# Two more ways to ScalarE and new weights for a planned instruction order (attention, FFN and gated FFN on one core)

## The chip, the cores and the metric

The kernel runs on one core of a Trainium2 chip. The metric is the device time of one execution in microseconds (us). The core has a matrix engine (TensorE: PE for its matmuls, PEld for its weight loads), and three engines for elementwise work: VectorE (DVE), ScalarE (ACT) and GpSimd (POOL). All transfers are issued from SyncE's queue (SP).

## The reference

Three layers follow each other, in double or single precision as the inputs come:

```python
# attention: q, k, v are (2, 8, 768, 64), proj is (64, 6)
mask   = bucket(q @ proj > 0) == bucket(k @ proj > 0)      # 6 sign bits make a bucket
scores = where(mask, q @ k.T / 8, -1e9)
attn   = exp(scores - max);  attn /= attn.sum(-1) + 1e-9
x      = attn @ v                                          # then (1536 tokens, 512)
# FFN 1: w_in (512, 2048), w_out (2048, 512)
h = x @ w_in;  g = max(h, 0) + log1p(exp(-abs(h)));  y = g @ w_out
# FFN 2: w_gate, w_val (512, 1536), w_out (1536, 512)
g = y @ w_gate;  out = (g * sigmoid(g) * (y @ w_val)) @ w_out
```

## The kernel before

**Chunks.** The 1536 tokens are cut into four chunks of 384 tokens: batch 0 gives chunks 0 and 1, batch 1 gives chunks 2 and 3. Attention goes head by head; a visit of a head and a chunk is three tiles of 128 queries by 768 keys. When a chunk's eight heads are done its x is split, turned by transfers and given to FFN 1 (`ffn1`, 16 blocks of 128 columns of w_in, then four blocks of y). FFN 2 (`ffn2`) comes last, for all chunks. Products are taken as three f16 matmuls of high and low parts, so nearly every tensor is split into `hi` and `lo` on the elementwise engines. The weights come as 64-bit numbers and are converted in pieces: three integer passes on DVE (lines 394, 399, 405), a square for the scale (432), high part (438 or 444) and low part (448). There are 8 pieces of w_in, 8 of w_out, 12 of w_gate and w_val, 6 of the last w_out.

**A tile of attention** (`units_of`). PE makes the scores and the mask in one product (776). `mx` on DVE copies them to SBUF and takes their maximum (787), and then works out the offset of the exponent in one element a row, `st[1] = st[0] * inv + 2` (792). `ex` on ACT takes the exponential with this offset (797). In chunk 0 (kind F, 24 tiles) the result is turned on PE (831), copied by ACT or DVE (862) and multiplied in f32 (870). In the other chunks (kind D, 72 tiles) it is split into `hi` (ACT 804, POOL 812 or DVE) and `lo` (817, POOL or DVE), turned by a transfer (PT<-P), and multiplied (854).

**Before a head's tiles** come three squares of k, q and v for their scales (`scales`: on ACT line 644, on DVE line 647), the split, the transfer that turns k and q, a copy of 64 rows (`cp`), and the hash bits (`planes`): a small product (574) whose signs become plus or minus the mask's constant, either in one DVE instruction (585), or with a Sign on ACT (594) and then an offset on POOL (599).

**FFN 1's block**: 12 matmuls into a bank of PSUM `f` (two of them in turn for batch 0); ACT takes the magnitude (`mag`, 1044), DVE the positive part (`relu`, 1049), ACT an exponential and a logarithm (1055, 1058), DVE adds (1061), then comes the split of g (ACT 1066 or POOL 1072; 1075). The bank is free when `mag` and `relu` have read it.

**The order is planned.** The program does not write its instructions in a fixed order. Each operation is a `Step` with an urgency (smaller is sooner) and one or several `ways`; a way is an engine, a length and sometimes a weight. `Order.run` plays the steps out with those lengths and emits them as it goes, and each engine then executes its own instructions in the order in which they were emitted. Three rules of it matter here:

```python
way = min(s.ways, key=lambda w: at(w) + (w[1] if w[0] != "D" else sum(w[1]) + 2.2) + (w[3] if len(w) > 3 else 0.0))
...
if w[0] in "WG":
    f += self.PORT * max(0.0, free.get("port", 0.0) - f)
...
(f for f in found if unit(f[2][0]) == unit(best[2][0]) and f[0] <= best[0] + self.SLACK),
key=lambda f: (f[1], f[0]),
```

A step takes the way with the smallest sum of start, length and weight. "V" and "W" are both DVE; a "W" or "G" (POOL) way is also pushed back by 0.75 of the time for which the plan holds the memory port of DVE and POOL taken (`PORT`). Among steps that could start on an engine within 0.1077 us of the earliest (`SLACK`), the most urgent goes first. The lengths are short formulas: with n elements a row, `dve(n)` = 0.08 + n/960, `stt(n)` = 0.13 + n/960, `act(n)` = 0.28 + n/1400, `gts(n)` = 0.05 + n/1050, `gps(n)` = 0.1 + n/510 us. `BV` holds the weights, `U` shifts of urgency, `GAP` the planned distance of tiles, `LEAD` how far ahead of its first tile a head's preparation is due, `W1_GAP` and `W2_GAP` the distance of the pieces of w_in and w_out.

Of the kernel before, what the change touches and what calls it, by code (L numbers as in the profile page):

```python
# [183 lines left out]
def tile_hash_attention__softplus_ffn__silu_glu(  # L184
# [51 lines left out]
    def pe(cols):  # L236
        return 0.04 + cols / 2400.0

    BV = dict(tf=1.0, th=1.091, hi=2.161, lo=0.772, slo=0.117, wlo=-0.43, bits=0.477, meas=0.564, cv=-0.593, ca=0.872)
    U = dict(vl=0, tp=-2.89, th=-2, tl=-2, w2=53.21, qp=-7.63, kp=-4.93, kv=3.56, f1=0, y=40, ev=-9.89, ex=3.56, hi=-7.89, lo=2.67, gw=423.98, x=2.84)  # L240

    const = ctx.enter_context(tc.tile_pool(name="const", bufs=1))
    xyp = ctx.enter_context(tc.tile_pool(name="xyp", bufs=1))
# [33 lines left out]
    def ways(urgency, opts, after=(), takes=(), uses=(), line=None):  # L277
        return order.step(urgency, opts, after, takes, uses, line)
# [357 lines left out]
    def scales(b, h, u, kv, ld_kv, qr, ld_q):  # L636

        n = NT * D
        m, x, inv = small(3), small(3), small(2)
        e = e_hd[b][:, 3 * h:3 * h + 3]  # L640
        src = (lambda: kv[0].t, lambda: qr.t, lambda: kv[1].t)

        def measure_a(i):
            return lambda: nc.scalar.activation(junk, src[i](), AF.Square, accum_out=m[:, i:i + 1])

        def measure_v(i):
            return lambda: nc.vector.scalar_tensor_tensor(
                out=junk2, in0=src[i](), scalar=1.0, in1=src[i](), op0=ALU.mult, op1=ALU.mult,
                accum_out=m[:, i:i + 1],
            )  # L650

        def least():
            nc.vector.scalar_tensor_tensor(
                out=e, in0=bank_.t[:, 8:11], scalar=2.0 ** 51, in1=floors, op0=ALU.mult, op1=ALU.max
            )

        def inverse():
            for i, c in enumerate((QK_SC, -QK_SC)):
                nc.vector.tensor_scalar(
                    inv[:, i:i + 1], e[:, 0:1], e[:, 1:2], c, op0=ALU.mult, op1=ALU.mult  # L660
                )
        ms = [
            ways(u, [("A", act(n) + 0.15, measure_a(i)), ("V", stt(n) - 0.07, measure_v(i), BV["meas"])],
                 [ld], uses=[o])
            for i, (ld, o) in enumerate(((ld_kv[0], kv[0]), (ld_q, qr), (ld_kv[1], kv[1])))
        ]
        s, bank_ = total(u, m, 3, ms)
        s = es = step(u, "W", 0.55, both(
            lambda: half_bits(bank_.t[:, 8:11], bank_.t[:, 0:3]), least, lambda: two_over(x, e)
        ), [s], uses=[bank_])  # L670
        iv = step(u + 5, "V", 0.4, inverse, [s])
        return dict(x=x, es=es, inv=inv, iv=iv, ready=s)

    def key_side(b, h, u, hs, raw, ld, proj_ready):

        nat, kk = Slot("natk"), Slot("k")
        n = NT * D

        def parts():
            if nat.t is None:  # L680
                new(att, [128, NT, 128], F16, nat)
            return (raw[0].t.rearrange("p (t d) -> p t d", d=D), nat.t[:, :, 0:64], nat.t[:, :, 64:128],
                    hs["x"][:, 0:1])

        def trans():
            a = new(att, [128, 2, NT * 128], F16, kk)
            nc.sync.dma_start_transpose(
                out=a[:, 0].rearrange("p (t c) -> p t c", c=128), in_=nat.t.rearrange("p t c -> p (t c)")
            )

        def copy_d():
            nc.sync.dma_start(out=kk.t[64:128, 1], in_=kk.t[0:64, 0])

        def copy_v():
            nc.vector.tensor_copy(kk.t[64:128, 1], kk.t[0:64, 0])

        def copy_a():
            nc.scalar.copy(kk.t[64:128, 1], kk.t[0:64, 0])

        g = step(u, "-", 0.0, lambda: None, [hs["ready"], ld[0]], takes=[nat], line="natk")  # L700
        lk = split(u, n, parts, [g], [raw[0], nat])
        tr = step(u, "D", (1.2, 0.95), trans, [lk], takes=[kk], uses=[nat], line="tk")
        cp = ways(u, [("W", dve(NT * 128, 4), copy_v, BV["cv"]), ("A", act(NT * 128), copy_a, BV["ca"]),
                      ("D", (0.68, 0.28), copy_d)], [tr], uses=[kk])
        pl = planes(u + U["kp"], 0, 2, lambda: kk.t[:, 0], lambda: kk.t[:, 1], [tr, proj_ready], [], [kk])
        return dict(k=kk, raw_v=raw[1], ready=[tr, cp] + pl, f_ready=ld[1])
# [13 lines left out]
    def query_side(b, h, half, u, hs, raw, ld, proj_ready):  # L720
# [22 lines left out]
        def copy_a():  # L743
# [2 lines left out]
        g = step(u, "-", 0.0, lambda: None, [hs["ready"], ld], takes=[nat], line="natq")  # L746
        lo = split(u, n, parts, [g], [raw, nat])
        tr = step(u, "D", (1.2, 0.48), trans, [lo], takes=[qq], uses=[nat], line="tq")
        cp = ways(u, [("W", dve(CN, 4), copy_v, BV["cv"]), ("A", act(CN), copy_a, BV["ca"]),
                      ("D", (0.68, 0.14), copy_d)], [tr], uses=[qq])  # L750
        pl = planes(u + U["qp"], 1, 1, lambda: qq.t[:, 0], lambda: qq.t[:, 1], [tr, proj_ready], [], [qq])
        return dict(q=qq, ready=[tr, cp] + pl)
# [6 lines left out]
    def units_of(b, h, half, due, hs, kd, qd):  # L759
# [7 lines left out]
        for t in range(HT):  # L767
# [13 lines left out]
            def mx(t=t, z=z, st=st, E=E):  # L781


                if t == 0:
                    new(att, [128, 2, HT], F32, sums)
                a = new(att, [128, 4], F32, st)
                nc.vector.tensor_scalar(  # L787
                    new(att, [128, 2, HS], F32, E), z.t[:, :, 0:HS], MASK_FLOOR, None,
                    op0=ALU.max, op1=ALU.max, accum_out=a[:, 0:1],
                )  # L790

                nc.vector.tensor_scalar(  # L792
                    a[:, 1:2], a[:, 0:1], hs["inv"][:, 1:2], E_SHIFT, op0=ALU.mult, op1=ALU.add
                )

            def ex(t=t, st=st, E=E):
# [68 lines left out]
            def apply_f(t=t, PT=PT):  # L865
# [3 lines left out]
                for kk in range(NT):  # L869
# [4 lines left out]

            s = step(u, "E", pe(4 * HS), qk, kd["ready"] + qd["ready"], takes=[z], uses=[kd["k"], qd["q"]],
                     line="qk", behind=turned[-2:-1])
            s = step(u, "V", dve(S) + 0.36, mx, [s, first, hs["iv"]],
                     takes=[st, E] + ([sums] if t == 0 else []), uses=[z] + ([sums] if t else []), line="mx")
            first = first or s
            s = x = step(u + U["ex"], "A", act(S) + 0.39, ex, [s], uses=[E, st, sums], line="ex")  # L880
            if kinds[t] == "D":
                s = ways(u + U["hi"], [("A", act(S), hi_a), ("G", gts(S) + 0.08, hi_g), ("W", dve(S, 2), hi_v, BV["hi"])], [s],
                         takes=[P], uses=[E], line="hi")
                s = ways(u + U["lo"], [("G", gps(S) + 0.05, lo(nc.gpsimd)), ("W", dve(S), lo(nc.vector), BV["lo"])], [s], uses=[E, P])
                s = step(u, "D", (1.72, 1.9), tr, [s], takes=[PT], uses=[P], line="tr")
            else:
                s = step(u + U["tp"], "E", 6 * 0.14, turn, [s], takes=[T], uses=[E], line="tp")
# [34 lines left out]
            )  # L922

        u += U["ev"]
        a = step(u, "G", 0.15, ev2a, [x], uses=[sums])
        a = step(u, "V", 0.17, ev2b, [a], uses=[sums])
        f = xn_open.get(c)
        s = step(u, "V", dve(HT * 64) + 0.07, ev3, [s, a, f], takes=[] if f else [xn[c]],
# [95 lines left out]
    def ffn1(c, due, x_ready, w1_ready, g_ready, w2_ready, y_ready):  # L1024
# [3 lines left out]
        for m in range(K1):  # L1028
# [19 lines left out]
            def relu(gi=gi, f=f, fr=fr):  # L1048
# [2 lines left out]
                    op0=ALU.mult, op1=ALU.max,  # L1051
                )

            def ex(fa=fa):
                nc.scalar.activation(fa.t, fa.t, AF.Exp, scale=-1.0)

# [23 lines left out]
                         x_ready + [w1_ready[gi], s], takes=[] if p else [f, g], uses=[f, g] if p else [], line="f1")  # L1080
            hs.append(s)
            a = step(U["f1"], "A", act(CN), mag, [s, g_ready], takes=[fa], uses=[f])
            r = step(U["f1"], "V", stt(CN) + 0.07, relu, [a, g_ready], takes=[fr], uses=[f])
            a = step(U["f1"], "A", act(CN) - 0.04, ex, [a], uses=[fa])
            a = step(U["f1"], "A", act(CN) + 0.04, ln, [a], uses=[fa])
            a = step(U["f1"], "W", stt(CN) + 0.07, add, [a, r], uses=[fa, fr])
# [116 lines left out]
    s, pm_bank = total(0, pm, 1, [s])  # L1203
    pjr = step(0, "V", 1.8, prep_proj, [s], uses=[pm_bank])

    T0, GAP, LEAD, W1_GAP, W2_GAP = 12, 2.611, 14.38, 5.974, 6.601


    visits = [(0, h, (0,), False) for h in range(H)]
# [135 lines left out]
```

## Time and profile before

| | |
|---|---|
| median of 3 runs | 885.31 us (883.08 to 885.72) |
| the profiled execution, its own time | 884.34 us |
| its span, first to last instruction | 882.5 us |
| busy of the span: PE, DVE, ACT, POOL | 779.3, 584.9, 460.3, 407.7 us |
| mean granted clock of TensorE | 0.957 of full speed |

Busy time is the time in which an engine executes an instruction, counted once where two overlap. Since the layers follow each other, a share of the whole span is a mean over stages with different limits. The time around the span (884.34 less 882.5, or 1.84 us) belongs to the execution and not to the program's instructions.

### The profile page before, as it was taken

Reading aid. Unit: us, or ns where it says so; the run is one execution under the profiler, and the core shown is the slowest. Engines: PE = TensorE matmul, PEld = TensorE weight load, DVE = VectorE, ACT = ScalarE, POOL = GpSimd, SP = SyncE. Lnnn points to the kernel's source line nnn. Section 1 sums busy time; section 2 is a strip of 40 time slices with the busy share of each in tenths; the row PEclk is TensorE's granted clock in tenths of the full one; section 3 lists DMA queues with packets and bytes.
Section 4 is the critical chain, followed back from the end, with each engine's and each line's share of the span. In section 5 each row is a group of like instructions: output and inputs, shape, how many; then the busy total and the mean of one; then the engine's idle time right before and its main releaser. Section 6 shows DMA issues by size and latency. Waiting matters only on the chain.

```text
span 882.5 us, 14634 instructions
## 1 busy us (share of the span) xinstructions
PE 779.3 (88%) x5462; PEld 505.3 (57%) x5462; DVE 584.9 (66%) x1157; ACT 460.3 (52%) x847; POOL 407.7 (46%) x430
## 2 busy tenths in 40 slices
PE   3787776877889886779999999899999999999998
PEld 1565654444445553445566666555576676677666
DVE  4798888789989899999667799968911311220320
ACT  4666667668567688767568548624411211211220
POOL 2345346877578788877348418512311210210220
PEclk9988998889879998899999999999999999999999
DMA  6445457946668787857793541342200000000000
GB/s 186 124 146 167 112 131 172 189 100 149 117 135 162 159 139 146 151 98 135 120 157 70 185 161 40 127 160 96 96 12 25 1 9 28 1 1 36 1 1 36
DMA packets 195048, 90.05 MB, mean 102 GB/s; under 512 B 156640, under 2 KB 181664, under 8 KB 194976
## 3 DMA queue, kind: packets, MB, share of 16 engines
q1 hardware_dynamic: 194976, 89.11, 43.0%
q8 instruction: 43, 0.70, 0.3%
q14 instruction: 29, 0.24, 0.1%
HBM read 47.35 MB, written 3.15 MB: 57 GB/s over the span
## 4 chain that ended last, share of the span: by engine, by line
PE 49%; DVE 22%; DMA 10%; POOL 7%; issue 6%; ACT 3%; SPq 1%; DVEq 0%; POOLq 0%; ACTq 0%
PE z L1020 8%; PE z L1022 8%; PE z L1021 8%; DMA PT<-P 4%; PE f L1183 4%; PE f L1181 4%; PE f L1182 4%; DVE E L787 3%; DVE fr L1061 2%; DMA q<-natq 2%; POOL P L817 2%; DVE fr L1049 2%; PE z L776 2%; DVE w32b L399 1%; PE y L1020 1%
## 5 line engine op out<-in xcount | busy, mean ns | idle before, releaser
L1149 DVE SCALAR_TENSOR_TENSOR sg<-z,smalls,sg 128x384 f32<-128x384 f32 x96 | 59.2, 616 | 176.9 <-ACT sg L1143 175.4
L1158 POOL TENSOR_TENSOR sT<-sg,sT 128x384 fp32r<-128x384 f32 x48 | 51.8, 1080 | 217.0 <-ACT sT L1155 211.1
L797 ACT ACTIVATE E<-E,st,smalls 128x768 f32<-128x768 f32 x96 | 98.1, 1022 | 28.0 <-DVE st L792 25.8
L776 PE MATMUL z<-k,q 128*128 128x384 f16 x384 | 87.6, 359 | 15.7 <-DVE E L787 15.4
L787 DVE TENSOR_SCALAR_CACHE_REDUCE E<-z 128x768 f32<-128x768 f32 x96 | 91.2, 950 | 9.4 <-POOL P L817 5.3
L817 POOL TENSOR_TENSOR P<-E,P 128x768 f16<-128x768 f32 x51 | 87.0, 1708 | 12.7 <-ACT P L804 9.8
L1075 POOL TENSOR_TENSOR g<-fr,g 128x384 f16<-128x384 f32 x64 | 73.6, 1154 | 16.7 <-ACT g L1066 13.1
L1020 PE MATMUL f<-xy,w1h 128*128 128x384 f16 x192 | 65.8, 343 | 10.7 <-DVE fr L1049 9.1
L854 PE MATMUL pv<-v,PT 128*128 128x64 f16 x1296 | 52.4, 197 | 19.1 <-DMA PT<-P 18.4
L854 PEld LDWEIGHTS <-PT 128*128 128x128 f16 x1296 | 47.6, 101 | 34.5 <-DMA PT<-P 27.4
L1021 PE MATMUL f<-xy,w1h 128*128 128x384 f16 x192 | 65.6, 342 | 0.0
L1022 PE MATMUL f<-xy,w1l 128*128 128x384 f16 x192 | 65.4, 341 | 0.0
L1020 PE MATMUL z<-xy,wgh 128*128 128x384 f16 x192 | 62.6, 326 | 0.7 <-DVE sg L1149 0.7
L1020 PE MATMUL z<-xy,wvh 128*128 128x384 f16 x192 | 62.6, 326 | 0.0
L1021 PE MATMUL z<-xy,wvh 128*128 128x384 f16 x192 | 62.6, 326 | 0.0
L1022 PE MATMUL z<-xy,wvl 128*128 128x384 f16 x192 | 62.6, 326 | 0.0
L1022 PE MATMUL z<-xy,wgl 128*128 128x384 f16 x192 | 62.6, 326 | 0.0
L1021 PE MATMUL z<-xy,wgh 128*128 128x384 f16 x192 | 62.6, 326 | 0.0
L776 PEld LDWEIGHTS <-q 128*128 128x128 f16 x384 | 36.3, 106 | 45.5 <-issue 24.5
L1143 ACT ACTIVATE sg<-z,smalls 128x384 f32<-128x384 f32 x48 | 27.8, 580 | 63.6 <-PE z L1022 63.5
L1061 DVE SCALAR_TENSOR_TENSOR fr<-fa,smalls,fr 128x384 f32<-128x384 f32 x64 | 55.4, 869 | 7.8 <-ACT fa L1058 5.4
L1155 ACT ACTIVATE sT<-sg 128x384 fp32r<-128x384 f32 x48 | 25.1, 522 | 61.8 <-DVE sg L1149 61.6
(189 smaller groups left out, 2032.0 us busy)
## 6 DMA issues: line engine op xcount, KB each, us to landing
raw64a<-in_moe_w_in_dram SPq DMA_DIRECT2D x16, 512.0 KB, 4.6
raw64a<-in_moe_w_out_dram SPq DMA_DIRECT2D x16, 512.0 KB, 5.0
raw64b<-in_moe_w_gate_dram SPq DMA_DIRECT2D x12, 512.0 KB, 4.3
raw64b<-in_moe_w_val_dram SPq DMA_DIRECT2D x12, 512.0 KB, 4.9
raw64b<-in_moe_w_out_dram SPq DMA_DIRECT2D x12, 512.0 KB, 4.3
rawk<-in_k_dram SPq DMA_DIRECT2D x19, 192.0 KB, 2.7
rawv<-in_v_dram SPq DMA_DIRECT2D x19, 192.0 KB, 3.3
rawq<-in_q_dram SPq DMA_DIRECT2D x16, 192.0 KB, 3.0
```

The lines of the kernel that those rows point to most:

```text
L776: nc.tensor.matmul(a[:, x, 0:HS], lhsT=qd["q"].t[:, w, ts], rhs=kd["k"].t[:, w, x * HS:(x + 1) * HS], start=(w == 0), stop=(w == 1),)
L787: nc.vector.tensor_scalar(new(att, [128, 2, HS], F32, E), z.t[:, :, 0:HS], MASK_FLOOR, None, op0=ALU.max, op1=ALU.max, accum_out=a[:, 0:1],)
L797: nc.scalar.activation(E.t, E.t, AF.Exp, bias=st.t[:, 1:2], scale=hs["inv"][:, 0:1], accum_out=sums.t[:, 0, t:t + 1],)
L817: return lambda: eng.tensor_tensor(P.t[:, 1, :], E.t.rearrange("p a b -> p (a b)"), P.t[:, 0, :], op=ALU.subtract)
L854: nc.tensor.matmul(pv.t[:, t, :], lhsT=PT.t[:, w, kk, :], rhs=values.t[:, kk, c0:c0 + D], start=(kk == 0 and w == 0 and c0 == 0), stop=(kk ...
L1020: nc.tensor.matmul(ps, lhsT=wh, rhs=xh, start=first, stop=False)
L1021: nc.tensor.matmul(ps, lhsT=wh, rhs=xl, start=False, stop=False)
L1022: nc.tensor.matmul(ps, lhsT=wl, rhs=xh, start=False, stop=last)
L1061: nc.vector.scalar_tensor_tensor(out=fr.t, in0=fa.t, scalar=sc[b]["sg"], in1=fr.t, op0=ALU.mult, op1=ALU.add)
L1075: return lambda: eng.tensor_tensor(g.t[:, 1], fr.t, g.t[:, 0], op=ALU.subtract)
L1149: return lambda: nc.vector.scalar_tensor_tensor(out=sg.t, in0=z.t[:, j, 0:CN], scalar=gvs[b, "gv"[j]][:, gi:gi + 1], in1=sg.t, op0=ALU.mul ...
L1158: return lambda: eng.tensor_tensor(sT.t[:, 1, :], sg.t, sT.t[:, 0, :].bitcast(F32), op=ALU.subtract)
```

## The change

Two steps get a second way, one step changes its kind, and a set of numbers changes; no arithmetic of the result is left out.

- The offset of the exponent is cut out of `mx` and becomes a step of its own, with the choice of DVE (as before) or ACT (`base_a`, an Identity with scale and bias, weight `st` = -0.497).
- The positive part in FFN 1 gets ACT as a second way (`relu_a`, a Relu with the same scale, weight `re` = 0.644).
- The DVE way of the squares counts as a user of the port ("W"), and its length goes from `stt(n)` - 0.07 to `stt(n)` + 0.14.
- Four lengths in the plan grow: the copies `cp` by 0.07 and 0.08, the DVE way of attention's `lo` by 0.07, the sums' `ev2a` from 0.15 to 0.25.
- The weights `BV` change: hash bits on DVE from 0.477 to -0.398, `hi` on DVE from 2.161 to 2.476, the pieces' `lo` on DVE from -0.43 to 0.431, squares on DVE from 0.564 to 0.422, `th` from 1.091 to 0.794 (used by a kind of tile that this kernel does not have).
- Urgencies and gaps change: `LEAD` from 14.38 to 11.412, `W2_GAP` from 6.601 to 10.599, and the shifts in `U`.

```diff
-    BV = dict(tf=1.0, th=1.091, hi=2.161, lo=0.772, slo=0.117, wlo=-0.43, bits=0.477, meas=0.564, cv=-0.593, ca=0.872)
-    U = dict(vl=0, tp=-2.89, th=-2, tl=-2, w2=53.21, qp=-7.63, kp=-4.93, kv=3.56, f1=0, y=40, ev=-9.89, ex=3.56, hi=-7.89, lo=2.67, gw=423.98, x=2.84)
+    BV = dict(re=0.644, st=-0.497, tf=1.0, th=0.794, hi=2.476, lo=0.772, slo=0.117, wlo=0.431, bits=-0.398, meas=0.422, cv=-0.593, ca=0.872)
+    U = dict(st=0, vl=0, tp=6.94, th=-2, tl=-0.28, w2=53.21, qp=-12.65, kp=-6.06, kv=-1.19, f1=0, y=40, ev=-9.03, ex=6.25, hi=-7.89, lo=1.9, gw=433.31, x=4.6)
...
+    shift = small()
+    nc.vector.memset(shift, E_SHIFT)
...
-            ways(u, [("A", act(n) + 0.15, measure_a(i)), ("V", stt(n) - 0.07, measure_v(i), BV["meas"])],
+            ways(u, [("A", act(n) + 0.15, measure_a(i)), ("W", stt(n) + 0.14, measure_v(i), BV["meas"])],
...
+            def base_v(st=st):
                 nc.vector.tensor_scalar(
-                    a[:, 1:2], a[:, 0:1], hs["inv"][:, 1:2], E_SHIFT, op0=ALU.mult, op1=ALU.add
+                    st.t[:, 1:2], st.t[:, 0:1], hs["inv"][:, 1:2], E_SHIFT, op0=ALU.mult, op1=ALU.add
+                )
+
+            def base_a(st=st):
+                nc.scalar.activation(
+                    st.t[:, 1:2], st.t[:, 0:1], AF.Identity, bias=shift, scale=hs["inv"][:, 1:2]
                 )
...
-            s = step(u, "V", dve(S) + 0.36, mx, [s, first, hs["iv"]],
+            s = step(u, "V", dve(S) + 0.15, mx, [s, first, hs["iv"]],
...
+            s = ways(u + U["st"], [("V", 0.21, base_v), ("A", 0.37, base_a, BV["st"])], [s], uses=[st], line="st")
...
+            def relu_a(gi=gi, f=f, fr=fr):
+                nc.scalar.activation(
+                    new(gpool, [128, CN], F32, fr), f.t[:, 0:CN], AF.Relu, scale=sc[b]["invg"][:, gi:gi + 1]
+                )
...
-            r = step(U["f1"], "V", stt(CN) + 0.07, relu, [a, g_ready], takes=[fr], uses=[f])
+            r = ways(U["f1"], [("V", stt(CN) + 0.08, relu), ("A", act(CN) + 0.04, relu_a, BV["re"])], [a, g_ready], takes=[fr], uses=[f])
...
-    T0, GAP, LEAD, W1_GAP, W2_GAP = 12, 2.611, 14.38, 5.974, 6.601
+    T0, GAP, LEAD, W1_GAP, W2_GAP = 12, 2.611, 11.412, 5.884, 10.599
```

## Rows read from the trace of the kernel before

**Rows 1.** Busy time by stage; columns: us, engine busy (instructions), granted clock, DMA share

```profile
0.00:160.00 160.00, 112.11 (x693) 80.80 (x694) 127.05 (x331) 102.48 (x195) 73.00 (x91) 0.91 0.56 149
160.00:420.00 260.00, 214.87 (x1932) 127.89 (x1930) 236.14 (x486) 185.44 (x351) 201.29 (x213) 0.92 0.71 139
420.00:640.00 220.00, 213.37 (x1543) 131.25 (x1542) 175.85 (x267) 124.51 (x217) 95.53 (x90) 0.99 0.45 121
640.00:882.50 242.50, 238.96 (x1299) 165.38 (x1297) 45.88 (x75) 47.90 (x86) 37.89 (x38) 1.00 0.04 14
```

**Rows 2.** The page's chain that ended last, shares of the span by engine

```profile
PE 49%; DVE 22%; DMA 10%; POOL 7%; issue 6%; ACT 3%; SPq 1%; DVEq 0%; POOLq 0%; ACTq 0%
```

**Rows 3.** PE's waits from 160 to 420 us: total us, times, longest

```profile
PE pv L854 <- DMA PT<-P: 13.9, 13, 2.8
PE z L776 <- DVE E L787: 11.9, 11, 2.1
PE f L1020 <- DVE fr L1049: 8.7, 8, 3.2
```

**Rows 4.** PE's waits from 420 to 640 us

```profile
PE z L1020 <- DVE fr L1049: 2.2, 1, 2.2
...
PE f L1020 <- DVE fr L1049: 0.4, 1, 0.4
```

**Rows 5.** Groups by line, whole span: count, busy us, mean ns, idle before and releasers

```profile
L797 ACT ACTIVATE E<-E,st,smalls 128x768 f32<-128x768 f32 x96 | 98.1, 1022 | 28.0 <-DVE st L792 25.8 <-DVE f L357 0.8 <-POOL k L599 0.6
...
L804 ACT CAST P<-E 128x768 f16<-128x768 f32 x51 | 42.2, 827 | 24.8 <-DMA PT<-P 24.6
...
L594 ACT ACTIVATE hb<-f,smalls 64x384 f16<-64x384 f32 x59 | 32.8, 570 | 24.3 <-PE f L574 20.5 <-POOL natq L553 2.0 <-POOL xp L553 0.9
...
L1049 DVE TENSOR_SCALAR fr<-f,smalls 128x384 f32<-128x384 f32 x48 | 29.2, 609 | 4.9 <-ACT fa L1044 3.8 <-POOL g L1075 0.8
...
L1044 ACT ACTIVATE fa<-f,smalls 128x384 f32<-128x384 f32 x48 | 27.6, 578 | 20.4 <-PE f L1022 14.9 <-DVE fr L1061 4.0 <-DVE fr L1049 0.4
...
L792 DVE TENSOR_SCALAR st<-st,smalls 128x1 f32<-128x1 f32 x96 | 20.5, 214 | 3.4
...
L1066 ACT CAST g<-fr 128x384 f16<-128x384 f32 x31 | 15.6, 504 | 7.5 <-DVE fr L1061 7.3
...
L585 DVE TENSOR_SCALAR k<-f,smalls 64x384 f16<-64x384 f32 x6 | 3.9, 656 | 0.0
...
L644 ACT ACTIVATE junk<-rawq 128x384 bf16<-128x384 f32 x6 | 3.1, 520 | 5.3 <-DMA rawq<-in_q_dram 5.3
```

**Rows 6.** Offset, line 792, by stage

```profile
0.00:160.00 160.00, 6.20 (x29) 0.91 0.56 149
160.00:420.00 260.00, 11.77 (x55) 0.92 0.71 139
```

**Rows 7.** Positive part, line 1049, by stage

```profile
160.00:420.00 260.00, 19.48 (x32) 0.92 0.71 139
420.00:640.00 220.00, 19.51 (x32) 0.99 0.45 121
```

**Rows 8.** Squares on DVE, line 647 (two records for each), by stage

```profile
0.00:160.00 160.00, 2.50 (x8) 0.91 0.56 149
160.00:420.00 260.00, 21.93 (x36) 0.92 0.71 139
```

**Rows 9.** Signs on ACT, line 594, by stage

```profile
0.00:160.00 160.00, 13.91 (x25) 0.91 0.56 149
160.00:420.00 260.00, 18.27 (x33) 0.92 0.71 139
```

**Rows 10.** All ACT_TABLE_LOAD groups: count, busy, mean ns

```profile
L305 ACT ACT_TABLE_LOAD x1 | 1.3, 1283 | 0.8 <-PEq L1329 0.8
L1143 ACT ACT_TABLE_LOAD x1 | 1.3, 1283 | 3.4 <-PE z L1022 3.4
```

**Rows 11.** Low part of w_out: min, median, max ns; first and last start, us

```profile
L1022 PE MATMUL y<-g,w2l x128: 324/326/528, 230.9 to 455.5; 128*128 128x384 f16 x128
...
L448 DVE SCALAR_TENSOR_TENSOR w2l<-w32a,smalls,w2h x8: 1274/1284/1920, 116.4 to 255.2; 128x1024 f16<-128x1024 f32 x8
```

More of the change, by code (lines that the diff above doesn't have):

```diff
@@ L702, in key_side @@
         tr = step(u, "D", (1.2, 0.95), trans, [lk], takes=[kk], uses=[nat], line="tk")
-        cp = ways(u, [("W", dve(NT * 128, 4), copy_v, BV["cv"]), ("A", act(NT * 128), copy_a, BV["ca"]),
+        cp = ways(u, [("W", dve(NT * 128, 4) + 0.07, copy_v, BV["cv"]), ("A", act(NT * 128), copy_a, BV["ca"]),
                       ("D", (0.68, 0.28), copy_d)], [tr], uses=[kk])
@@ L748, in query_side @@
         tr = step(u, "D", (1.2, 0.48), trans, [lo], takes=[qq], uses=[nat], line="tq")
-        cp = ways(u, [("W", dve(CN, 4), copy_v, BV["cv"]), ("A", act(CN), copy_a, BV["ca"]),
+        cp = ways(u, [("W", dve(CN, 4) + 0.08, copy_v, BV["cv"]), ("A", act(CN), copy_a, BV["ca"]),
                       ("D", (0.68, 0.14), copy_d)], [tr], uses=[qq])
@@ L883, in units_of @@
                          takes=[P], uses=[E], line="hi")
-                s = ways(u + U["lo"], [("G", gps(S) + 0.05, lo(nc.gpsimd)), ("W", dve(S), lo(nc.vector), BV["lo"])], [s], uses=[E, P])
+                s = ways(u + U["lo"], [("G", gps(S) + 0.05, lo(nc.gpsimd)), ("W", dve(S) + 0.07, lo(nc.vector), BV["lo"])], [s], uses=[E, P])
                 s = step(u, "D", (1.72, 1.9), tr, [s], takes=[PT], uses=[P], line="tr")
@@ L924, in units_of @@
         u += U["ev"]
-        a = step(u, "G", 0.15, ev2a, [x], uses=[sums])
+        a = step(u, "G", 0.25, ev2a, [x], uses=[sums])
         a = step(u, "V", 0.17, ev2b, [a], uses=[sums])
```

## The prediction

> **What bounds the kernel now.** I read the busy time by stage first, because the layers follow each other [rows 1]. The reader is to see four stages. From 640 us on (D) PE is busy for 238.96 of 242.5 us at full clock and no other engine for more than 47.90: nothing that this change touches runs there, so D stays as it is. From 420 to 640 us (C) PE is busy for 213.37 of 220 us; 6.6 us are all that a faster VectorE could win. From 160 to 420 us (B: attention of chunks 1 to 3 beside FFN 1 of chunks 0 and 1) DVE is busy for 236.14 of 260 us (0.91), POOL for 0.77, ACT for 0.71, and PE is idle for 45 us. In the first 160 us (A: chunk 0 and the pieces of w_in) DVE has 0.79, ACT 0.64, POOL 0.46, and PE is idle for 48 us. So time is to be had in A and B alone, and the busiest engine there is DVE.
>
> Next the chain that ended last [rows 2]: PE 49%, DVE 22%, DMA 10%, ACT 3%. D alone makes 27% of the span, all of it PE, so ahead of D, DVE and PE have about equal shares. Then what ended PE's waits in B [rows 3]: DVE 11.9 + 8.7 = 20.6 us, the transfers that turn P 13.9 us. So a DVE that has less to do shortens about 20.6 of these 34.5 us, or 0.6 of them; the transfers do not follow from DVE alone. I shall count half of what DVE saves or gains in A and B as time.
>
> **The change, part by part.** How often each new way is taken the trace cannot show: the plan decides by the rule quoted ahead. I work out the point at which it turns, and bound the counts by none and all.
>
> *The offset.* DVE's 0.21 stands against ACT's 0.37 - 0.497 = -0.127, so ACT is taken unless it could start more than 0.34 us after DVE. The instruction takes 0.214 us on DVE [rows 5]. On ACT the trace has no such row. The casts of 768 and 384 elements (827 and 504 ns) give 0.841 ns for an element, and the exponential, which also has a scale and a bias by row, takes 1022 ns at 768 elements, so at one element 1022 - 767 x 0.841 = 377 ns, an estimate from rows 5. In 24 of 96 cases ACT sat idle for the offset (the count of that wait in the same view), for 25.8 us in all [rows 5]: those go to ACT surely. I take 19 of 29 in A and 35 of 55 in B [rows 6]. DVE: 19 x 0.214 = 4.1 and 35 x 0.214 = 7.5 us less; ACT: 7.2 and 13.2 us more. Bounds for B: from 24/96 of 55, 3.0 us, to all, 11.8 us. Queued behind the ACT instruction is its own exponential, which waits for it: per tile the way from maximum to exponential grows by 377 - 214 = 163 ns.
>
> *The positive part.* DVE's 0.61 stands against ACT's 0.594 + 0.644 = 1.238, so ACT is taken where DVE could start more than 0.63 us after ACT. As DVE is the fuller engine in B, I take half of 32 there, and 10 of 32 in C, where DVE is less full [rows 1, 7]. DVE loses 16 x 0.609 = 9.7 us in B and 6.1 in C; ACT gains 16 x 0.578 = 9.2 us, by the price of the magnitude, which has the same shape, source and scale [rows 5]. Bounds for B: nothing to 19.5 us. It also frees the PSUM bank sooner, for which PE waited 8.7 us in B [rows 3].
>
> The Trainium skill, page "ScalarE: Activation LUTs", section "Rules for kernel authors", speaks against this edit: relu belongs on VectorE, which it puts at up to about three times as fast per element in bf16. The rows do not bear it out for f32 out of PSUM, where the magnitude on ACT takes 578 ns and the positive part on DVE 609 [rows 5]; by the rule, the 16 in B would cost ACT up to 16 x 1.83 = 29 us in place of 9.2, and the sum would lose all of B's gain.
>
> *The squares.* DVE's side goes from 0.46 + 0.564 = 1.024 to 0.67 + 0.422 = 1.092 against ACT's 0.704, and is now pushed back while POOL is planned on the port, and POOL is busy 0.77 of B [rows 1]. One on DVE takes 21.93/18 = 1.22 us there [rows 8], on ACT 0.52 and a read of its sum [rows 5], which I put at 0.71 with the plan. I take 10 of B's 18: DVE 12.2 us less, ACT 7.1 more. Bounds: none to 21.9 us. A has only 4 on DVE; I leave them.
>
> *The hash bits.* This goes the other way. DVE was taken if it could start 0.54 us sooner than ACT (0.62 + 0.477 against 0.554); now it is taken even if it starts 0.33 us later (0.62 - 0.398). 25 in A and 33 in B are on ACT [rows 9]; I take 12 of each back to DVE at 0.656 us [rows 5]: 7.9 us more for DVE in A and in B, ACT 12 x 0.570 = 6.8 less in each. Bounds: none, to 16.4 us in A and 21.6 in B. POOL loses its second half of the work, too.
>
> *Lengths, urgencies, gaps.* The longer lengths of `cp`, `lo` and `ev2a` add no instruction. Urgency only ranks steps that could start within 0.11 us of each other, which matters on a full queue, DVE's in B. `LEAD` lets a head's loads come due 3.0 us later; no load is added, SP's queue issues the same ones. I cost these at nothing: what hides a later load is that the raw tiles are loaded as soon as their buffer is free. If that cover is gone, a head waits up to those 3.0 us. The pieces' `lo` turns from 1.197 - 0.43 to 1.197 + 0.431 on DVE against 3.33 on POOL; DVE still has to be 1.7 us behind to lose one, so I leave all on DVE. `W2_GAP` makes the last piece of w_out due 7 x 4.0 = 28 us later (a rival, below).
>
> *The sum.* A: DVE -4.1 + 7.9 = +3.8 us, half is +1.9. B: -7.5 - 9.7 - 12.2 + 7.9 = -21.5 us, half is -10.8. ACT in B goes to 185.4 + 13.2 + 9.2 + 7.1 - 6.8 = 208 us of then 249, or 0.84, still under DVE's 0.86. C: of PE's idle time 2.2 + 0.4 us waited for the positive part [rows 4]; I take 1. D: nothing. Together -9.9 us. From the profiled execution's own 884.34 us that gives 874.4; this execution lay 0.97 us under the median of the runs, 885.31, so 875.4, and I say 875. With every unknown at its end: A between -2.0 (29 x 0.214 = 6.2 less, 2.5 of squares less, bits stay: -8.7, half -4.4) and +8.2; B between -26.6 (-11.8 - 19.5 - 21.9, halved) and +9.3 (+21.6 - 3.0, halved). That would be some 852 to 903 us; both ends need all choices to fall one way, so the range takes in about half of each side.
>
> **The rivals.** A measurement of this kernel tells 0.3% (2.7 us) from no change.
>
> *ACT takes DVE's place, time as before: 13%.* ACT gets the offset, the positive part and squares, all in front of exponentials and casts of the same queue. For it: the 13.9 us of waits on transfers, which start only after casts and low parts, do not go away with DVE's work [rows 3]. Against it: ACT would be at 0.84 and has 3% of the chain [rows 2]. Time: 883 to 888 us. The Trainium skill's rule on relu, quoted above from "ScalarE: Activation LUTs", would end here if it held for this form.
>
> *Slower through the hash bits: 16%.* In A the positive part is not there to be moved, so the bits that return to DVE meet only the 6.2 us of offsets that can leave [rows 6]. From 10 of 25 bits on (10 x 0.656 = 6.6 us) DVE has more work in A than before. With all 25: +16.4 - 4.1 = +12.3 us in A; if A is paid in full, as DVE stood at 0.79 there, and B's bits (+21.6) eat its gain (29.4 us) to 7.8, half counted, the time is 885.3 + 12.3 - 3.9 = about 894 us. Against it: a DVE bit spares the path Sign, then POOL, about 0.9 us for a head's keys and queries.
>
> *Slower through late w_out: 9%.* The low parts of w_out ran from 116.4 to 255.2 us, and the first product that needs them started at 230.9 [rows 11], so y already begins before the last piece is through. If the 28 us later due time of the last piece is carried over by a third, PE loses about 9 us in B: with the forecast's gain 884, without it 894 us.
>
> *A larger gain: 6%.* Most squares and positive parts move and the bits stay: -20 us or more, 865 or less.
>
> *Identity or Relu need another function table: 1%.* The trace has two table loads, at the start and at FFN 2's sigmoid, of 1283 ns each [rows 10]; magnitude, Sign, Square, Exp and Ln share the first. If the two new functions did not, 60 moved steps with two loads each would cost 154 us.
>
> **How the numbers follow.** The forecast itself, a gain of 3 to 18 us, has 55% and its own range of 867 to 882 us. With the larger gain, faster has 61%; same has 13%; slower 16 + 9 + 1 = 26%. The range reaches from 863 (half of the larger gains) to 891 us (most of the two slower rivals), and leaves out less than 2 in 10.
>
> **What would show it.** In the changed kernel's profile: Identity and Relu rows on ACT, at about 0.38 and 0.58 us; fewer rows of lines 792, 1049 and 647 on DVE and more of 585; in the stage up to the last exponential DVE's busy time 15 to 20 us lower and ACT's about 25 higher; the end of attention about 10 us sooner; PE's waits on the positive part under 8.7 us; D of unchanged length. I am wrong if DVE's busy time falls and the end of attention does not come sooner (then transfers, ACT or the order itself bound B), if DVE's busy time does not fall (bits), or if y starts later than 230.9 us beside idle PE.

## The result and the profile after

The changed kernel takes 871.93 us (median of 4 runs, 870.49 to 873.61) against 885.51 us: a ratio of 0.9847, 95% interval 0.9808 to 0.9885, or 13.6 us less. The profiled execution has a span of 868.8 us, 13.7 less than before; all rows here show one execution of a kernel, and the executions of one kernel differ by 1 to 14 us. Busy time by the stages of [rows 1] (columns as there: PE, PEld, DVE, ACT, POOL, granted clock, DMA share):

```profile
0.00:160.00 160.00, 118.07 (x682) 83.96 (x682) 128.06 (x319) 100.25 (x203) 59.51 (x83) 0.85 0.55 148
160.00:420.00 260.00, 216.68 (x2063) 131.43 (x2062) 225.52 (x447) 194.96 (x400) 210.55 (x205) 0.95 0.75 145
420.00:640.00 220.00, 213.63 (x1485) 133.97 (x1484) 165.36 (x246) 121.02 (x214) 90.51 (x87) 1.00 0.42 115
640.00:868.80 228.80, 225.09 (x1238) 153.93 (x1236) 44.51 (x72) 46.79 (x84) 35.89 (x36) 1.00 0.04 15
```

Stages with fixed ends compare different work once something moves. So I cut both spans at two events: the start of the 24th exponential, the last of chunk 0, and the start of the first magnitude of FFN 1 in chunk 2, from where on PE hardly waits. The kernel before, cut there:

```profile
0.00:134.20 134.20, 94.94 (x580) 70.08 (x580) 106.87 (x292) 84.94 (x165) 52.24 (x74) 0.94 0.52 147
134.20:459.70 325.50, 269.75 (x2448) 163.11 (x2449) 280.91 (x579) 226.98 (x420) 237.91 (x245) 0.92 0.73 141
459.70:882.50 422.80, 414.62 (x2436) 272.13 (x2434) 197.13 (x286) 148.41 (x263) 117.56 (x112) 1.00 0.18 58
```

And the changed kernel:

```profile
0.00:135.30 135.30, 101.16 (x589) 73.85 (x590) 107.80 (x281) 83.24 (x173) 45.38 (x68) 0.86 0.52 144
135.30:447.00 311.70, 258.69 (x2423) 157.46 (x2423) 260.38 (x513) 229.95 (x461) 239.69 (x232) 0.95 0.75 147
447.00:868.80 421.80, 413.61 (x2454) 271.96 (x2452) 195.28 (x290) 149.83 (x267) 111.39 (x112) 1.00 0.19 59
```

The reader is to see that the first part is 1.1 us longer, the middle 13.8 us shorter, and the rest 1.0 us shorter, and that DVE's busy time in the middle fell by 20.5 us, while ACT's and POOL's rose by 3.0 and 1.8. PE's columns say more. Its idle time (the length less PE's busy time) fell by only 2.7 us in the middle, from 55.8 to 53.0; the other 11.1 us are busy time, at a mean granted clock of 0.95 of full speed in place of 0.92 (the mean is over time at the clock's two levels, 2.4 and 1.2 GHz). In the first part it was the other way: 5.1 us less idle, 6.2 us more busy, at 0.86 in place of 0.94. Both parts together have 7.9 us less idle time and 4.8 us less busy time. What moved is in the groups by line of the changed kernel (count, busy us, mean ns, idle before):

```profile
L825 POOL TENSOR_TENSOR P<-E,P 128x768 f16<-128x768 f32 x65 | 115.3, 1776 | 35.2 <-ACT P L812 32.6 <-POOL sum L917 0.5 <-POOL xp L555 0.4
...
L1058 DVE TENSOR_SCALAR fr<-f,smalls 128x384 f32<-128x384 f32 x48 | 29.3, 609 | 5.9 <-POOL g L1089 3.4 <-ACT fa L1053 2.3
...
L800 ACT ACTIVATE st<-st,smalls 128x1 f32<-128x1 f32 x65 | 24.8, 382 | 31.8 <-DVE E L789 31.3
...
L587 DVE TENSOR_SCALAR k<-f,smalls 64x384 f16<-64x384 f32 x33 | 21.6, 663 | 5.7 <-PE f L576 5.4
...
L587 DVE TENSOR_SCALAR q<-f,smalls 64x384 f16<-64x384 f32 x25 | 16.7, 667 | 9.7 <-PE f L576 9.4
...
L1058 DVE TENSOR_SCALAR fr<-z,smalls 128x384 f32<-128x384 f32 x16 | 9.8, 611 | 5.0 <-POOL g L1089 2.4 <-ACT fa L1053 1.3 <-ACT fa L1072 1.3
...
L825 DVE TENSOR_TENSOR P<-E,P 128x768 f16<-128x768 f32 x7 | 8.8, 1264 | 0.3
...
L596 ACT ACTIVATE hb<-f,smalls 64x384 f16<-64x384 f32 x12 | 6.8, 570 | 2.1 <-PE f L576 2.0
...
L795 DVE TENSOR_SCALAR st<-st,smalls 128x1 f32<-128x1 f32 x31 | 6.4, 207 | 0.5
...
L649 DVE SCALAR_TENSOR_TENSOR junk<-rawv 128x384 bf16<-128x384 f32 x1 | 0.5, 540 | 0.0
```

65 of 96 offsets are on ACT at 382 ns. All 64 positive parts are still on DVE (48 and 16, line 1058), and no Relu row exists: the new way was never taken. 58 hash bits are on DVE in place of 11. One square is left on DVE in place of 22. And something that the sum did not have: POOL takes 65 of attention's low parts in place of 51, DVE 7 in place of 21 (22.4 us before, 8.8 now).

### The profile page after: what moved, and what is told of

Same layout as the page of the kernel before. It is cut to its first block, busy times and chain, and to the rows that moved or that the text cites. A ratio compares the mean times of both kernels' runs of the same rounds, so it can differ in the third digit from the quotient of the medians.

```text
span 868.8 us, 14540 instructions
## 1 busy us (share of the span) xinstructions
PE 773.5 (89%) x5462; PEld 503.3 (58%) x5462; DVE 563.4 (65%) x1083; ACT 463.0 (53%) x899; POOL 396.5 (46%) x411
## 5 line engine op out<-in xcount | busy, mean ns | idle before, releaser
L825 POOL TENSOR_TENSOR P<-E,P 128x768 f16<-128x768 f32 x65 | 115.3, 1776 | 35.2 <-ACT P L812 32.6
L778 PE MATMUL z<-k,q 128*128 128x384 f16 x384 | 86.7, 356 | 21.5 <-DVE E L789 21.4
L1089 POOL TENSOR_TENSOR g<-fr,g 128x384 f16<-128x384 f32 x64 | 71.6, 1122 | 12.5 <-ACT g L1080 8.5
L862 PE MATMUL pv<-v,PT 128*128 128x64 f16 x1296 | 50.4, 194 | 22.6 <-DMA PT<-P 22.5
L862 PEld LDWEIGHTS <-PT 128*128 128x128 f16 x1296 | 45.3, 99 | 38.1 <-DMA PT<-P 31.9
L1029 PE MATMUL f<-xy,w1h 128*128 128x384 f16 x192 | 64.2, 334 | 2.5 <-DVE fr L1058 1.9
L1030 PE MATMUL f<-xy,w1h 128*128 128x384 f16 x192 | 64.0, 333 | 0.0
L1031 PE MATMUL f<-xy,w1l 128*128 128x384 f16 x192 | 63.6, 331 | 0.0
L1195 PE MATMUL f<-woh,sT 128*128 128x512 f32 x144 | 56.6, 393 | 0.0
```

The source lines that it names most:

```text
L778: nc.tensor.matmul(a[:, x, 0:HS], lhsT=qd["q"].t[:, w, ts], rhs=kd["k"].t[:, w, x * HS:(x + 1) * HS], start=(w == 0), stop=(w == 1),)
L825: return lambda: eng.tensor_tensor(P.t[:, 1, :], E.t.rearrange("p a b -> p (a b)"), P.t[:, 0, :], op=ALU.subtract)
L862: nc.tensor.matmul(pv.t[:, t, :], lhsT=PT.t[:, w, kk, :], rhs=values.t[:, kk, c0:c0 + D], start=(kk == 0 and w == 0 and c0 == 0), stop=(kk ...
L1029: nc.tensor.matmul(ps, lhsT=wh, rhs=xh, start=first, stop=False)
L1030: nc.tensor.matmul(ps, lhsT=wh, rhs=xl, start=False, stop=False)
L1031: nc.tensor.matmul(ps, lhsT=wl, rhs=xh, start=False, stop=last)
```

## The experiments

Each time is a median beside runs of the kernel before on the same chip; the ratio is to those, with its 95% interval. Two kinds of kernel are used. In the first kind the plan stays as it is in one of the two kernels, and a table, made from the other kernel's plan, says on which engine a step's instruction is emitted, at the place where it stood. In the second kind one part of the change is made or undone and the plan is run anew, as the change itself does.

The first kind shares this edit:

```diff
-            fn()
+            emit(s, eng, fn)
...
+def emit(s, eng, fn):
+    table = SWAP.get(s.kind[0]) if s.kind else None
+    if table:
+        want = table[s.kind[1]]
+        if s.kind[0] == "bits":
+            return (s.on_v if want == "V" else s.on_a)()
+        if s.kind[0] == "then":
+            return
+        fn = next(w[2] for w in s.ways if w[0].replace("W", "V") == want)
+    fn()
```

**Order against engines.** The order of before with all engines of the changed kernel, and the counterpart:

```diff
+SWAP = {"bits": ..., "gh": ..., "ph": ..., "pl": ..., "sh": ..., "sl": ..., "sq": ..., "st": ..., "wh": ...}
```

> Every instruction stands where the plan of before put it, but the offsets, squares, hash bits and splits run on the engine that the plan of the changed kernel chose. Theory 1 (the gain is the work that left DVE): nearly the whole gain is there, 870 to 877 us, with DVE busy for about 563 us in place of 585. Theory 2 (the gain is the new order, by urgencies and gaps): 882 to 888 us, as before, although DVE's busy time falls.

> The counterpart: every instruction stands where the plan of the changed kernel put it, but the same steps run on the engines of before (all offsets on DVE). Theory 1: 880 to 888 us, the gain is gone, DVE busy for about 585 us. Theory 2: 870 to 876 us, the gain stays.

Measured: 922.9 us, ratio 1.0424 (1.0388 to 1.0461), and 919.7 us, 1.0382 (1.0347 to 1.0417). Neither theory expected that. Cut at the same two events, the middles of the order of before with the new engines, and of its counterpart, are:

```profile
145.70:498.30 352.60, 275.65 (x2450) 165.12 (x2451) 240.33 (x509) 234.40 (x469) 243.36 (x238) 0.90 0.69 130
149.40:490.70 341.30, 269.23 (x2441) 162.65 (x2441) 275.27 (x582) 221.23 (x413) 230.57 (x240) 0.93 0.69 135
```

In the first, DVE is busy for 240.3 us, 40.6 less than before and the least of all kernels here, and the stretch is 27.1 us longer. PE is idle for 77.0 and 72.1 us, against 55.8 before. So both theories fall as they stood: DVE's work by itself does not set the time, and the order by itself does not either. The likely reason, which no run here isolates: an instruction that is put on another engine at its old place stands in a queue that was planned without it, in front of instructions that others wait for.

**The squares alone**, order of before:

```diff
+SWAP = {"sq": "..."}   # 21 squares from DVE to ACT, none the other way
```

> The order of before, and only the 21 squares that the changed kernel has on ACT go there from DVE. DVE loses 21 of 22 squares of 24.4 us in all, or 23 us, and ACT gains 21 x 0.71 = 15 us. Theory 1, with half of DVE's saving counted as time: 872 to 880 us. Theory 2: 883 to 888 us.

Measured: 877.4 us, ratio 0.9906 (0.9871 to 0.9941), in the range of theory 1. The middle:

```profile
134.80:452.70 317.90, 265.21 (x2447) 162.65 (x2448) 269.38 (x545) 233.89 (x453) 237.69 (x245) 0.94 0.75 145
```

DVE is 11.5 us less busy in the middle than before and the stretch 7.6 us shorter. That is the one part whose gain shows by itself, though DVE's busy time fell by only half of the 23 us that left it: its other instructions became longer by the rest.

**The offsets alone**, order of before:

```diff
+SWAP = {"st": "..."}   # 65 offsets on ACT, 31 on DVE
```

> The order of before, and only the 65 offsets that the changed kernel has on ACT go there. DVE loses 65 x 0.214 = 14 us, ACT gains 65 x 0.38 = 25 us, and the way from maximum to exponential grows by 0.16 us a tile. Theory 1: 877 to 882 us. Theory 2: 883 to 888 us. If the longer way from maximum to exponential costs more than DVE saves: 887 us or more.

Measured: 894.0 us, 1.0085 (1.0051 to 1.0119), slower: DVE's work falls and time is lost, as the third expectation had it. The middle:

```profile
135.00:465.60 330.60, 269.25 (x2451) 163.36 (x2452) 267.93 (x532) 239.27 (x466) 241.01 (x244) 0.92 0.74 139
```

DVE is 13.0 us less busy there than before, and the stretch is 5.1 us longer.

**The hash bits alone**, order of before:

```diff
+SWAP = {"bits": "...", "then": "..."}   # 49 of 70 from ACT and POOL to DVE, 2 the other way
```

> The order of before, and only the hash bits go where the changed kernel has them: 51 of 70 change place, 49 from ACT and POOL to DVE, 2 the other way. DVE gains 47 x 0.66 = 31 us. By the prediction's pricing half of it is time: 895 to 905 us. If the short way over one instruction and the free POOL outweigh it: 878 to 887 us.

Measured: 893.5 us, 1.0102 (1.0069 to 1.0135), between the two expectations. The first two parts:

```profile
0.00:142.80 142.80, 104.07 (x583) 78.51 (x583) 114.57 (x313) 75.83 (x146) 34.62 (x55) 0.83 0.51 138
142.80:471.00 328.20, 271.88 (x2448) 163.26 (x2447) 286.51 (x607) 213.40 (x392) 220.60 (x216) 0.91 0.73 139
```

The first part, up to chunk 0's last exponential, is 8.6 us longer than before with DVE 7.7 us busier there: the place that the prediction's rival named. But PE is 9.1 us busier there too, with about the same products at a granted clock of 0.83 in place of 0.94. Over both parts PE's idle time is 95.0 us, as before, and the 11.3 us that were lost are PE's busy time. So the rows do not tell what DVE's bits cost from what the clock cost.

**The offsets, planned.**

```diff
-            s = ways(u + U["st"], [("V", 0.21, base_v), ("A", 0.37, base_a, BV["st"])], [s], uses=[st], line="st")
+            s = ways(u + U["st"], [("V", 0.21, base_v)], [s], uses=[st], line="st")
```

> The changed kernel without the ACT way of the offset, planned anew: 96 offsets on DVE. If the offset's move is part of the gain: 96 x 0.21 less 31 x 0.21 = 14 us more on DVE, half of it as time, 876 to 882 us. If the moved offset costs as much as it saves, as the run that moved it alone in the order of before suggests: 868 to 874 us.

Measured: 880.9 us, 0.9951 (0.9928 to 0.9975). Without the offsets' new way two thirds of the gain are gone. The same move that costs 0.85% in the order of before is part of the gain where the plan knows of it. The first two parts (of an execution of 885.4 us):

```profile
0.00:140.10 140.10, 104.16 (x584) 77.75 (x585) 111.67 (x300) 78.33 (x157) 53.71 (x69) 0.84 0.53 143
140.10:459.90 319.80, 267.53 (x2443) 164.04 (x2442) 255.68 (x554) 220.45 (x422) 240.44 (x228) 0.90 0.74 141
```

PE's idle time in them is 88.2 us, about the changed kernel's 87.2; its busy time is 11.8 us longer, at a lower clock. So the loss does not show as PE's waiting, and how the offsets bring it about stays open.

**The squares, planned**, on the kernel before:

```diff
-    BV = dict(..., meas=0.564, ...)
+    BV = dict(..., meas=0.422, ...)
...
-            ways(u, [("A", act(n) + 0.15, measure_a(i)), ("V", stt(n) - 0.07, measure_v(i), BV["meas"])],
+            ways(u, [("A", act(n) + 0.15, measure_a(i)), ("W", stt(n) + 0.14, measure_v(i), BV["meas"])],
```

> The kernel before with the edit of the squares alone (way W, length and weight of the changed kernel), planned anew. The plan moves 17 of 22 squares to ACT. If the squares are the core of the gain: 873 to 880 us, as where they were moved by themselves in the order of before (877 us). If their gain there was only that no other instruction moved, 883 to 888 us.

Measured: 882.6 us, 0.9982 (0.9966 to 0.9997), between the two expectations, and a fifth of what the squares gave in the fixed order.

**The hash bits, planned**, both ways:

```diff
 # the changed kernel
-bits=-0.398
+bits=0.477
 # the kernel before
-bits=0.477
+bits=-0.398
```

> The changed kernel with the weight of the hash bits as before, planned anew: about 47 bits more on ACT and POOL, 31 us less on DVE, 27 us more on ACT, 45 us more on POOL. By the prediction's pricing, which counts the bits on DVE as a loss: 860 to 868 us. If POOL is what the bits relieve, so that POOL can take the low parts of attention from DVE: 874 to 884 us.

> The kernel before with the weight of the hash bits alone changed, planned anew: 50 of 70 bits on DVE in place of 11, and by the plan 11 squares there in place of 22, with 7 more low parts on POOL. If bits on DVE are the core of the gain, because they free ACT and POOL for squares and low parts: 870 to 879 us. If they only gain together with the other edits: 882 to 890 us. By the prediction's pricing: 892 us or more.

Measured: 900.0 us, 1.0197 (1.0166 to 1.0228), for the changed kernel with the old weight, and 922.5 us, 1.0409 (1.0363 to 1.0455), for the kernel before with the new one. The first is far outside both of its ranges: taking the bits back off DVE, which the prediction's pricing counts as a gain, costs 28 us. The second is 30 us above the 892 us from which on the prediction's pricing had it, and far from the other two expectations. The first two parts of the latter (of an execution of 930.6 us):

```profile
0.00:151.80 151.80, 118.03 (x602) 87.11 (x602) 114.47 (x309) 77.66 (x152) 47.22 (x72) 0.78 0.49 137
151.80:496.90 345.10, 274.92 (x2500) 168.04 (x2499) 270.76 (x569) 219.29 (x407) 248.53 (x252) 0.88 0.72 140
```

and the middle of the former:

```profile
133.40:477.70 344.30, 278.69 (x2523) 168.80 (x2523) 258.88 (x505) 244.91 (x489) 255.25 (x248) 0.88 0.72 137
```

Both middles are about 345 us long with DVE at 0.75 to 0.78 and TensorE's granted clock at 0.88. In both, FFN 1 of chunk 0 drags: its 16th magnitude starts at 297 us with the old weight and at 331 us in the other, against 231 before and 245 in the changed kernel, so that FFN 1 is missing as work for PE beside attention and is done later. PE is idle for 65.6 and 70.2 us of the two middles, against 53.0 in the changed kernel.

**Urgencies and gaps** of before in the changed kernel:

```diff
-    U = dict(st=0, vl=0, tp=6.94, th=-2, tl=-0.28, w2=53.21, qp=-12.65, kp=-6.06, kv=-1.19, f1=0, y=40, ev=-9.03, ex=6.25, ...)
+    U = dict(st=0, vl=0, tp=-2.89, th=-2, tl=-2, w2=53.21, qp=-7.63, kp=-4.93, kv=3.56, f1=0, y=40, ev=-9.89, ex=3.56, ...)
...
-    T0, GAP, LEAD, W1_GAP, W2_GAP = 12, 2.611, 11.412, 5.884, 10.599
+    T0, GAP, LEAD, W1_GAP, W2_GAP = 12, 2.611, 14.38, 5.974, 6.601
```

> The changed kernel with the shifts of urgency, LEAD, W1_GAP and W2_GAP of before, planned anew. If urgencies and gaps only rank steps that are ready together, as the prediction costed them at nothing: 869 to 877 us. If they carry the gain: 882 to 890 us. If late w_out pieces cost time in the changed kernel, it is faster than the changed kernel, under 869 us.

Measured: 891.2 us, 1.0057 (1.0035 to 1.0079): the whole gain is gone and a little more. Its three parts:

```profile
0.00:145.60 145.60, 104.55 (x590) 76.04 (x590) 116.14 (x298) 85.78 (x174) 38.39 (x59) 0.84 0.52 145
145.60:461.70 316.10, 265.81 (x2433) 161.49 (x2433) 254.63 (x503) 225.73 (x455) 239.57 (x232) 0.92 0.75 141
461.70:889.70 428.00, 417.58 (x2447) 273.70 (x2443) 199.19 (x286) 148.16 (x266) 114.95 (x111) 0.99 0.18 57
```

Half of the loss against the changed kernel is in the first part (145.6 against 135.3 us). DVE is 8.3 us busier there, although it has as many hash bits in the first 135 us as in the changed kernel (21 and 22), so other work has come into that part. The first low part of w_out, for one, runs at 111.5 us under the old gaps and at 127.4 us in the changed kernel; whether that matters was not tried.

**The start shifted by 0.2 us**, which stands for no operation:

```diff
-    T0, GAP, LEAD, W1_GAP, W2_GAP = 12, 2.611, 11.412, 5.884, 10.599
+    T0, GAP, LEAD, W1_GAP, W2_GAP = 12.2, 2.611, 11.412, 5.884, 10.599
```

> The changed kernel with one number that stands for no operation moved a little: the planned start of the first tile, 12.2 us in place of 12. The plan comes out anew with nearly the same engines (70 offsets, 45 squares and 46 bits' worth of ACT, DVE and POOL within 6 of each kind). If the gain comes from where the work runs: 869 to 876 us, as the changed kernel. If it is this one order that is lucky: anywhere from 876 to 890 us, which would also say how far the planned runs can be read.

Measured: 872.9 us, 0.9847 (0.9822 to 0.9872), the same as the changed kernel, from another order of instructions. Its first two parts:

```profile
0.00:137.40 137.40, 96.13 (x589) 70.71 (x590) 108.10 (x282) 85.41 (x175) 41.53 (x66) 0.91 0.54 146
137.40:448.60 311.20, 264.63 (x2429) 163.24 (x2428) 258.04 (x518) 228.75 (x460) 230.71 (x219) 0.92 0.76 147
```

The lengths of 137.4 and 311.2 us stand beside 135.3 and 311.7, and PE's idle time in both parts together is 87.8 us beside 87.2. Inside the middle it is split in another way: 46.6 us idle and 264.6 busy, at 0.92, against 53.0 and 258.7 at 0.95. So in this one other plan the gain does not hang on one order of instructions; it stays as long as ways, weights and urgencies stay together.

**The positive part on ACT**:

```diff
-    BV = dict(re=0.644, ...)
+    BV = dict(re=0.0, ...)
```

> The changed kernel with the weight of the positive part's ACT way at 0 in place of 0.644, planned anew: 34 of 64 go to ACT, which none did. DVE loses 34 x 0.61 = 21 us, ACT gains 34 x 0.58 = 20 us, most of it while FFN 1 runs. By the prediction's pricing of 9.7 us of DVE for 16 in the stage from 160 to 420 us, half of it time: 864 to 870 us. If ACT is by now the engine that the tiles wait for: 873 us or more.

Measured: 886.2 us, 1.0001 (0.9975 to 1.0027): by its number in the second expectation, but not by its reason, since the parts with the tiles did not grow. The parts (of an execution of 882.4 us) show a price that had no place in the sum:

```profile
130.80:444.90 314.10, 258.39 (x2441) 157.56 (x2441) 252.87 (x515) 233.98 (x462) 236.00 (x230) 0.95 0.78 147
444.90:880.70 435.80, 417.39 (x2436) 272.71 (x2434) 189.80 (x264) 157.46 (x286) 122.85 (x115) 0.99 0.18 56
```

Relu runs at the expected length:

```profile
L1064 ACT ACTIVATE fr<-f,smalls 128x384 f32<-128x384 f32 x22 | 12.7, 578 | 4.5 <-POOL g L1089 4.2
...
L1064 ACT ACTIVATE fr<-z,smalls 128x384 f32<-128x384 f32 x12 | 6.9, 578 | 2.5 <-POOL g L1089 2.4
```

The first magnitude of chunk 2 starts at 444.9 us, 2.1 sooner than in the changed kernel, which is within the spread of executions, but the last part is 14.0 us longer than there. The waits of PE from 445 to 600 us in this kernel, then those of the changed kernel from 447 to 600 us:

```profile
PE f L1029 <- DVE smalls L359: 4.8, 2, 3.2
PE z L1029 <- ACT fr L1064: 3.8, 2, 2.3
PE f L347 <- ACT wvh L434: 2.6, 3, 1.1
PE f L347 <- DVE wgl L450: 1.8, 1, 1.8
...
PE z L1029 <- DVE sg L1163: 2.1, 1, 2.1
PE z L1029 <- DVE fr L1058: 1.4, 1, 1.4
PE pv L862 <- DMA PT<-P: 0.9, 1, 0.9
```

The first four, 13.0 us, name the Relu itself and the weight pieces; all waits listed for the changed kernel come to 4.4 us. No version here is faster than the changed kernel.

## Why the prediction was right, and where it was not

The time, 871.93 us, is 3.1 under the forecast of 875 and in its own range, and the sum's parts by place come close, when the parts cut at events stand for the stages: A +1.9 forecast and 1.1 measured, B -10.8 and -13.8, C and D together -1 and -1.0. So does DVE's relief in B, 21.5 us forecast and 20.5 measured. Attention ended 9.1 us sooner (its last exponential is over at 450.3 us, before at 459.4), and up to there DVE was busy for 17.7 us less; both signs had been named. But the agreement is in part luck: terms cancelled, one step was priced at nothing, one term had the wrong sign, and B's time is not where the sum looked for it.

**The step that failed is "Lengths, urgencies, gaps", which I costed at nothing.** Undoing urgencies and gaps alone takes the time from 871.9 to 891.2 us. The clean pair for the first part are these two kernels, with 22 and 21 hash bits of the first 135 us on DVE: chunk 0's last exponential starts at 135.3 and 145.6 us. The other plans fit, though they differ in more than the urgencies. With 22 or 23 bits there it starts at 130.8, 137.4 and 140.1 us under the new urgencies (the positive part on ACT, the shifted start, offsets on DVE); with 22 and 16 bits at 142.8 and 151.8 us under the old ones (bits alone in the order of before, bits alone planned). With two or three bits it starts at 133.4 us under the new (old weight of the bits) and at 134.2 under the old (the kernel before). So the rival "slower through the hash bits" had its place right, under the old urgencies. That the new ones kept it from coming true fits these rows but is not shown: in the clean pair DVE had more of other work, not more bits, and the clock of these parts goes from 0.78 to 0.94.

**The hash bits had the wrong sign.** The sum counts them as 7.9 us more for DVE in A and in B, half of it as time lost. In the changed kernel 47 of them moved to DVE, and putting them back costs 28 us (900.0 us). Their price depends on the rest of the plan, and the trace of the kernel before could not show it.

**A rival that stays:** the numbers may only fit together. Each single step away from the changed kernel lost time: 9.0 us for the offsets, 14.3 for the positive part, 19.3 for urgencies and gaps, 28.1 for the bits. So the loss without the new urgencies does not single them out. Against it stands one plan, the shifted start, which lost nothing.

**B's mechanism is only half borne out.** The sum let half of DVE's saving come off PE's waits. PE's idle time in the middle fell by 2.7 us of the 13.8, and by 9.2 of 14.3 in the kernel with the shifted start; the rest is PE's own busy time, at a granted clock that the sum had no term for. With the squares moved alone it is 3.1 of 7.6 us.

**Terms that were mis-sized.** Offsets: 65 moved where I took 54, at 382 ns where the estimate from rows 5 was 377. Positive part: none moved where I took 26: by the plan's own rule, its DVE was never 0.63 us behind its ACT when a positive part was due. Squares: 21 moved where I took 10; the whole-span saving is 24.4 to 0.6 us of DVE, against the 12.2 forecast. Hash bits: 47 moved where I took 24, so 7.2 to 38.3 us on DVE. With them 47 Signs left ACT, whose busy time from 160 to 420 us was put at 208 us and came out at 195.0. Low parts of P: not in the sum, 13.6 us off DVE and 28.3 onto POOL, which had lost its half of 47 bits; that the one made the other possible was only argued. The passes that convert w_in and w_out changed in length, though not in number: the first from a mean of 703 to 867 ns, the second from 1421 to 1267 and the third from 1599 to 1314:

```profile
L407 DVE SCALAR_TENSOR_TENSOR w32a<-raw64a,w32a x16: 1205/1226/1755, 13.6 to 255.9; 128x1024 int32<-128x1024 int32 x16
```

The third's median is that of before, 1226 ns, and the longest fell from 3915 to 1755 ns. The Trainium skill, page "SBUF — State Buffer", section "SBUF: two separate sides", says that a DVE instruction with two inputs in SBUF and a GpSimd instruction that reads SBUF lock each other out of a shared port for their whole length. The spread agrees with that, but no run here takes POOL's instruction away from beside this pass alone. One slip in the sum: A's lower end is written as -2.0, while its own working, and the 852 us, go by -4.4.

**Half of DVE's saving as time** was no law. In the middle of the changed kernel the stretch fell by 13.8 us where DVE's busy time fell by 20.5, and with the squares moved alone by 7.6 for 11.5, two thirds in both; where the offsets moved alone it had the other sign, and with all engines moved in the old order DVE was spared 40.6 us and 27.1 us were lost.

**The rivals.** ACT in DVE's place did not hold for the change; with the positive part moved too it did, in the last part of that kernel. The Trainium skill's rule that relu belongs on VectorE ("ScalarE: Activation LUTs", "Rules for kernel authors") was not borne out by the duration, 578 ns against 609 on DVE, for f32 out of PSUM. The move was still not worth it here, for PE's waits in the last part. Late w_out did not cost, as far as the rows tell: the fourth block of y was done 2.7 us later than before (line 1128 at 309.2 against 306.5 us), and the eighth 13.4 us sooner. But one sign of being wrong did come: the first product with w_out's low part started at 246.6 us, not by 230.9, and from 235 to 239 us PE sat idle. It was not w_out that held y back: `ffn1` puts it behind the products of all 16 blocks, and the 16th magnitude started at 245.4 us (before at 230.7), and PE's longest wait from 225 to 260 us, 4.3 us, was for a transfer of P. No table was loaded for Identity or Relu; the kernel with 60 Identities and 34 Relus has:

```profile
L305 ACT ACT_TABLE_LOAD x1 | 1.3, 1283 | 0.8 <-PEq L1343 0.8
L1157 ACT ACT_TABLE_LOAD x1 | 1.3, 1283 | 3.4 <-PE z L1031 3.4
```

**What the wait shows now.** In the stage from 160 to 420 us, PE's waits on the positive part are down from 8.7 to 1.9 us though no positive part moved. Those on the copies of the scores are up from 11.9 to 14.0, and those on P's transfers from 13.9 to 20.2 us:

```profile
PE pv L862 <- DMA PT<-P: 20.2, 19, 4.3
PE z L778 <- DVE E L789: 14.0, 13, 6.1
...
PE f L1029 <- DVE fr L1058: 1.9, 3, 1.3
```

So the freer DVE shows at FFN 1's banks alone. The three waits together went from 34.5 to 36.1 us in a stage that now holds other work, and the transfers of P stay the longest of them.

**What stays open.** Why FFN 1 of chunk 0 drags by 50 to 100 us in the two plans with changed bits was not settled: the instructions stand late in PE's order, and which of the plan's numbers puts them there was not tried. Which of the urgencies carries the gain was not told apart either, nor how much of each gain and loss is TensorE's clock: no run changes the clock alone.

## What to carry to other kernels

In a kernel whose order is planned, engines and order are one choice: the same move can gain where the plan is made with it and lose where it is not (the offsets), or the other way about (the squares gained more in the old order), so a part of such a change, measured alone, can have the other sign. Do not read the busy engine's saving as time, look where the next wait of PE lies, part a shorter stretch into PE's idle and busy time before calling it a saved wait, and cut the span at events (the last exponential of a chunk, the first product of the next layer) rather than at fixed times. An urgency that moves no work is not to be priced at nothing without a run.

## What the runs showed of the hardware

An Identity of one element a row with scale and bias takes 382 ns on ACT, against 207 to 214 ns for the same on DVE, so moving such a step takes nearly twice the time from the one engine that it gives back to the other. Relu of 128x384 from PSUM takes 578 ns on ACT, where DVE takes 609. The span of kernels that do the same work in other orders and on other engines went from 868.8 to 928.9 us, with a mean granted clock of TensorE of 0.959 and 0.911 of full speed at these two ends. In the two middles of 345 us, where PE was idle for 65.6 and 70.2 us, the clock stood at 0.88, and at 0.95 in the changed kernel, with 53.0 us idle. But the sum of idle time alone does not give the clock: in the first part it was 0.78 with 33.8 us idle (bits alone, planned), 0.86 with 34.1 (the changed kernel) and 0.94 with 39.3 (the kernel before).
